# Window attention and two MoE layers on one core: whole 32-bit float scores for every unit, and a first batch that keeps its probabilities and values whole

## The chip, the cores and the metric

One NeuronCore of a Trainium2 chip runs the whole program. The metric is the device time of one execution in microseconds; lower is better. Between two kernels of this size a difference of under 0.5% (some 4.6 us) counts here as no change.

## The reference, cut to what matters

```python
batch, n_heads, seq_l, seq_g, head_dim = 4, 8, 512, 32, 64      # window = 32
k_all, v_all = concat([k_g, k_l]), concat([v_g, v_l])           # along the rows
out_g = sm(scale * q_g @ k_all.T) @ v_all                       # 32 global rows see all rows
s_ll  = where(abs(i - j) <= window, scale * q_l @ k_l.T, -1e9)
s_lg  = scale * q_l @ k_g.T
out_l = sm(concat([s_lg, s_ll])) @ v_all                        # 512 local rows: band + global
x = concat([out_g, out_l])            # 4 * 544 = 2176 tokens of 8 * 64 = 512
x = maximum(maximum(x @ w1, x @ w2), x @ w3) @ w_out            # 512 -> 768 -> 512
x = (sigmoid(x @ w_gate) * (x @ w_val)) @ w_out2                # 512 -> 1536 -> 512
```

The attention is in 32-bit floats. The MoE weights arrive as 64-bit floats (two 32-bit words each) and are turned into 32-bit floats on the chip.

## The kernel before, in words

**Units and chunks.** The attention is cut into 32 units `t`: batch `b` (4), half of the 512 local rows (2), pair of heads `hp` (4). Four units make a chunk `c` (256 rows, and in every second half the 32 global rows too: 288 columns). Chunk `c` then goes through the first MoE layer: `moe1_l1` (18 weight tiles, w1, w2 and w3 by six blocks `f`) and `moe1_l2` (w_out, six tiles). After the eighth chunk the second MoE layer runs in six chunks of 384 columns.

**A float as two.** Most matmuls take a float as a high part and a rest, and sum three products (high x high, high x rest, rest x high: `TERMS`, `mm3`). Making such a pair costs a cast on ScalarE and a subtraction on VectorE or GpSimd. Only chunk 0's first layer (`WHOLE1`, `WHOLE2`) takes 32-bit floats whole (names `xw`, `hw`, `wraw`).

**A unit's steps.** `at_prep_rows` (units 0 to 7, from row-major q and k, turned by TensorE transposes `tq`, `tk`) or `at_prep_qk` (units 8 to 31, turned on VectorE) makes the pairs `qs` and `ks`. `at_scores` runs 12 matmuls of 64 rows x 224 columns into `sp` (two heads in the two halves of the array's rows), `at_scores_g` three of 256 columns into `sg` (and three of 32 in the first half). `at_softmax` gives `sm`, splits it into `pc` in 16-bit floats (three casts on ScalarE L604, three subtractions on VectorE L607) and has a DMA transpose it into `pt` (L610). `at_prep_v` splits the values in three 16-bit parts `vb` (ScalarE L509, GpSimd L511 and L515, VectorE L513). `at_av` multiplies: 40 matmuls of 64 columns and four of 256. For each pair of head pairs `at_softmax_g` and `at_av_g` do the same for the global rows (`pcg`, `ptg`, `og`).

**Order and buffers.** Every function is a generator of small steps, and the list `ORDER` says in which order all steps of the program are emitted. Each engine and each DMA queue takes its instructions strictly in that order. All loads but chunk 0's k go through SyncE's queue (SP), and so do the DMA transposes, so that one waiting there holds up the loads behind it. The pool `slot` has `NSLOT` = 25 buffers of 4 KB per partition; it holds q, k and v rows of the first batch (`qn`, `kn`, `kx`, `vrg`), raw weights (`wraw`) and weight pairs (`w`), 24 of the latter in the end. `conv_w` loads a weight tile (L224, L227) and turns it into floats (L231 to L240). Chunk 0 uses the raw tile; the pair is made from it afterwards (L246, and a subtraction on GpSimd under L218).

## Time and profile before

| what | value |
|---|---|
| time, median of 3 runs (lowest, highest) | 913.1 us (911.05, 914.78) |
| the profiled execution: time, span of its trace | 913.18 us, 911.5 us |
| TensorE busy (matmul) | 849.0 us, 93% of the span |
| VectorE, ScalarE, GpSimd busy | 455.5, 436.6, 295.4 us |
| share of TensorE in the chain that ended last | 78% |

The span is the time from the first to the last instruction of the profiled execution. A busy share is an average over stages with different limits, and a matmul's busy time includes its latency, so back-to-back matmuls overlap in it. `L12` is line 12 of the kernel.

### The profile page before, as it was taken

The page shows a single profiled execution, that of the slowest core. Times are in us where ns is not written, and L with a number is a line of the kernel's source. Part 1 is how long each engine was busy: PE and PEld are TensorE (multiplying, and loading weights), DVE is VectorE, ACT ScalarE, POOL GpSimd, SP SyncE. Part 2 cuts the span into 40 slices and gives each one's busy share as a digit, 9 for nine tenths or more (in the row PEclk, how much of TensorE's full clock was granted, in tenths as well). Part 3 has the DMA queues.
Part 4 walks back from the last instruction along what each step waited for, and adds up shares of the span by engine and source line. Part 5 has one row for each costly group of instructions (what it writes and reads, how often), then busy time and mean ns, then how long its engine had stood idle before and what let it go on. Part 6 is the DMA issues. An engine that isn't in the chain of part 4 may idle for free.

```text
span 911.5 us, 18123 instructions
## 1 busy us (share of the span) xinstructions
PE 849.0 (93%) x7004; PEld 786.1 (86%) x7004; DVE 455.5 (50%) x1092; ACT 436.6 (48%) x1141; POOL 295.4 (32%) x284
## 2 busy tenths in 40 slices
PE   0759959999999998999999999999999999999998
PEld 0547749899999998999999999999999999999997
DVE  4797967776577776855476673121111111111211
ACT  4776658676666766664596753221211211211122
POOL 4554427644545463624265653000100100000000
PEclk9988989999999999999999999999999999999999
DMA  7687744566553646645777210000100200000000
GB/s 210 130 185 205 174 80 85 102 97 104 101 97 85 105 91 116 119 88 122 246 260 244 88 34 31 33 29 9 61 1 1 64 1 1 13 36 1 1 35 24
DMA packets 205031, 79.91 MB, mean 88 GB/s; under 512 B 171792, under 2 KB 200464, under 8 KB 204944
## 3 DMA queue, kind: packets, MB, share of 16 engines
q1 hardware_dynamic: 202288, 78.09, 36.5%
q8 instruction: 55, 0.90, 0.4%
q10 hardware_dynamic: 2656, 0.66, 0.4%
q14 instruction: 32, 0.26, 0.1%
HBM read 54.59 MB, written 8.91 MB: 70 GB/s over the span
## 4 chain that ended last, share of the span: by engine, by line
PE 78%; DVE 7%; DMA 6%; ACT 4%; SPq 2%; issue 2%; POOL 0%; DVEq 0%; POOLq 0%; ACTq 0%
PE acc L861 16%; PE ps L261 8%; PE ps L263 7%; PE ps L262 7%; PE pg L262 5%; PE pg L263 5%; PE pg L261 5%; PE pv L261 5%; PE pv L263 5%; PE pv L262 5%; DMA wraw<-in_moe_w_dram 3%; PE ot L659 2%; PE sp L538 2%; DVE pc L607 1%; DVE wraw L240 1%
## 5 line engine op out<-in xcount | busy, mean ns | idle before, releaser
L261 PE MATMUL ps<-xt,w 128*128 128x288 f32 (+1 forms) x504 | 150.1, 298 | 2.5 <-ACT h L744 1.7
L861 PE MATMUL acc<-w,gt 128*128 128x512 f32 x612 | 150.6, 396 | 0.0
L263 PE MATMUL ps<-xt,w 128*128 128x288 f32 (+1 forms) x504 | 147.2, 292 | 0.0
L262 PE MATMUL ps<-xt,w 128*128 128x288 f32 (+1 forms) x504 | 146.0, 290 | 0.1
L861 PEld LDWEIGHTS acc<-w,gt 128*128 128x128 f32 x612 | 114.1, 188 | 23.7
L846 ACT CAST gt<-sig 128x384 fp32r<-128x384 f32 (+1 forms) x72 | 35.7, 496 | 173.5 <-PE acc L861 124.2
L848 DVE TENSOR_TENSOR gt<-sig,gt 128x384 fp32r<-128x384 f32 (+1 forms) x72 | 41.7, 582 | 152.6 <-ACT gt L846 152.6
L843 DVE TENSOR_TENSOR sig<-pv,sig 128x384 f32<-128x384 f32 (+1 forms) x72 | 38.1, 534 | 155.3 <-PE pv L263 118.9
L218 POOL TENSOR_TENSOR w<-wraw,w 128x512 fp32r<-128x512 f32 x60 | 83.1, 1397 | 78.2 <-ACT w L246 74.7
L218 POOL TENSOR_TENSOR x<-x2r,x 128x384 fp32r<-128x384 f32 (+1 forms) x24 | 25.7, 1077 | 253.4 <-ACT x L824 253.4
L261 PEld LDWEIGHTS ps<-xt,w 128*128 128x128 f32 x504 | 95.4, 189 | 7.9 <-ACT h L744 2.6
L262 PEld LDWEIGHTS ps<-xt,w 128*128 128x128 f32 x504 | 95.5, 190 | 0.5 <-DVE xt L725 0.3
L263 PEld LDWEIGHTS ps<-xt,w 128*128 128x128 f32 x504 | 95.3, 189 | 0.0
L261 PE MATMUL pv<-x,w 128*128 128x384 f32 (+1 forms) x288 | 93.9, 326 | 0.4 <-DVE sig L843 0.4
L263 PE MATMUL pv<-x,w 128*128 128x384 f32 (+1 forms) x288 | 93.9, 326 | 0.0
L263 PE MATMUL pg<-x,w 128*128 128x384 f32 (+1 forms) x288 | 93.9, 326 | 0.0
L262 PE MATMUL pg<-x,w 128*128 128x384 f32 (+1 forms) x288 | 93.9, 326 | 0.0
L262 PE MATMUL pv<-x,w 128*128 128x384 f32 (+1 forms) x288 | 93.9, 326 | 0.0
L261 PE MATMUL pg<-x,w 128*128 128x384 f32 (+1 forms) x288 | 93.9, 326 | 0.0
L607 DVE TENSOR_TENSOR pc<-sm,pc 64x512 f16<-64x512 f32 (+1 forms) x96 | 69.7, 726 | 5.5 <-ACT pc L604 4.2
L841 ACT ACTIVATE sig<-pg 128x384 f32<-128x384 f32 (+1 forms) x72 | 33.8, 473 | 76.9 <-PE pg L263 42.7
L575 ACT ACTIVATE sm<-sm,st 128x224 f32<-128x224 f32 x128 | 60.7, 477 | 8.9 <-DVE st L544 8.8
(124 smaller groups left out, 1785.5 us busy)
## 6 DMA issues: line engine op xcount, KB each, us to landing
wraw<-in_moe_w_dram SPq DMA_DIRECT2D x18, 512.0 KB, 4.9
wraw<-in_moe_w_out_dram SPq DMA_DIRECT2D x18, 512.0 KB, 4.6
wraw<-in_moe_w_gate_dram SPq DMA_DIRECT2D x12, 512.0 KB, 5.8
wraw<-in_moe_w_val_dram SPq DMA_DIRECT2D x12, 512.0 KB, 8.4
vr<-in_v_l_dram SPq DMA_DIRECT2D x48, 96.0 KB, 2.5
out_dram<-o SPq DMA_DIRECT2D x17, 256.0 KB, 2.2
x2d<-x2s SPq DMA_DIRECT2D x32, 128.0 KB, 2.4
x2r<-x2d SPq DMA_DIRECT2D x20, 192.0 KB, 2.5
```

The lines of the kernel that those rows point to most:

```text
L218: nc.gpsimd.tensor_tensor(out=out, in0=a, in1=f32(b), op=ALU.subtract)
L261: nc.tensor.matmul(ps, lhsT=wh, rhs=xh, start=first, stop=False)
L262: nc.tensor.matmul(ps, lhsT=wh, rhs=xl, start=False, stop=False)
L263: nc.tensor.matmul(ps, lhsT=wl, rhs=xh, start=False, stop=last)
L538: nc.tensor.matmul(sp[hh][:, j, 0:224], lhsT=qs[r, a, qc], rhs=ks[r, k, kc], start=(i == 0), stop=(i == 2))
L575: nc.scalar.activation(sm4[:, i], sm4[:, i], AF.Exp, bias=st[:, 0, i:i + 1], scale=-1.0, accum_out=st[:, 2, i:i + 1])
L607: nc.vector.tensor_tensor(out=l_, in0=s_, in1=h_, op=ALU.subtract)
L841: nc.scalar.activation(sg[:, 0:n], pg[:, 0:n], AF.Sigmoid)
L843: nc.vector.tensor_tensor(out=sg[:, 0:n], in0=pv[:, 0:n], in1=sg[:, 0:n], op=ALU.mult)
L846: nc.scalar.copy(gt[:, 0, 0:n], sg[:, 0:n])
L848: nc.vector.tensor_tensor(out=gt[:, 1, 0:n], in0=sg[:, 0:n], in1=f32(gt[:, 0, 0:n]), op=ALU.subtract)
L861: nc.tensor.matmul(acc[ci, i], lhsT=gt[:, l, c], rhs=w[:, m], start=(f == 0 and l + m == 0), stop=(f == NF2 - 1 and l == 1))
```

## The change

It does five things.

- **Scores (all units).** `qs` and `ks` are whole 32-bit floats. Each score product is one matmul in place of three: `at_scores` has 4 in place of 12, `at_scores_g` 1 or 2 in place of 3 or 6. The pairs are not made any more: for units 0 to 7 a copy on VectorE and three on ScalarE take q and k out of PSUM, for units 8 to 31 the transposed tiles are used as they are.
- **First batch (units 0 to 7).** The probabilities stay whole floats. TensorE transposes them, eight 128 x 128 transposes a unit into two PSUM tiles `tp`; ScalarE copies one to SBUF, VectorE the other (`pw`). `at_av` is eight whole matmuls of 128 columns on the loaded values `vrg`; `at_prep_v` does nothing there. The global rows go the same way (five transposes, `at_av_gw`, 20 matmuls of 32 columns for a pair), with the values loaded once more (`at_load_vg`, `vrw`).
- **Loads.** The first batch's values are loaded in another layout, seven transfers for four heads in place of five.
- **`NSLOT`** is 26. Buffer counts of `qs`, `ks` go to 2 and 3.
- **`ORDER`** is a new list.

```diff
-    1857, 1858, 1859, 1860, 0, 1861, 1836, 1822, 1871, 1872, 1, 1823, 2, 1824, 1873, 1874, 1843, 1844, 1837, 3, 1838,
...
-    NSLOT = 4 * NF1 + 1
+    NSLOT = 4 * NF1 + 2
...
+    def at_load_vg(hp):
+        vr = at.tile([P, 5, 2, D], F32, tag="vb", name="vrw", bufs=3)
+        vl = v_l[0, 2 * hp:2 * hp + 2]
+        dma = nc.sync.dma_start
+        dma(out=vr[0:32, 0], in_=v_g[0, 2 * hp:2 * hp + 2].rearrange("h s d -> s h d"))
+        dma(out=vr[32:128, 0], in_=vl[:, 0:96, :].rearrange("h r d -> r h d"))
+        for hh in range(2):
+            dma(out=vr[:, 1:4, hh], in_=vl[hh, 96:480, :].rearrange("(k r) d -> r k d", r=P))
+        dma(out=vr[64:96, 4], in_=vl[:, 480:512, :].rearrange("h r d -> r h d"))
+        u[hp, "vrw"] = vr
...
-        qs = at.tile([P, 2, HS], F32R, tag="qs", name="qs")
-        nc.scalar.copy(qs[:, 0], tq[:, 0:HS])
-        yield
-        ks = at.tile([P, 2, 384], F32R, tag="ks", name="ks", bufs=2)
-        for o, i in parts(ks[:, 0, :]):
+        qs = at.tile([P, HS], F32, tag="qs", name="qw", bufs=2)
+        nc.vector.tensor_copy(qs, tq[:, 0:HS])
+        yield
+        ks = at.tile([P, 384], F32, tag="ks", name="kw", bufs=3)
+        for o, i in parts(ks):
             nc.scalar.copy(o, i)
-        yield
-        nc.vector.tensor_tensor(out=qs[:, 1], in0=tq[:, 0:HS], in1=f32(qs[:, 0]), op=ALU.subtract)
-        yield
-        for (o, i), (h, _) in zip(parts(ks[:, 1, :]), parts(ks[:, 0, :])):
-            nc.vector.tensor_tensor(out=o, in0=i, in1=f32(h), op=ALU.subtract)
...
-            for i, (a, k) in enumerate(TERMS):
-                for hh in range(2):
-                    r = slice(64 * hh, 64 * hh + 64)
-                    nc.tensor.matmul(sp[hh][:, j, 0:224], lhsT=qs[r, a, qc], rhs=ks[r, k, kc], start=(i == 0), stop=(i == 2))
+            for hh in range(2):
+                r = slice(64 * hh, 64 * hh + 64)
+                nc.tensor.matmul(sp[hh][:, j, 0:224], lhsT=qs[r, qc], rhs=ks[r, kc], start=True, stop=True)
...
+        if t < NGRP * NP:
+            tp = []
+            for hh in range(2):
+                tp.append(ps_o.tile([P, 2 * HS], F32, tag="ot", name="tp"))
+                for i in range(4):
+                    e = sm4[:, 2 * hh + i // 2, 96 * (i % 2):96 * (i % 2) + P]
+                    nc.tensor.matmul(tp[hh][:, P * i:P * i + P], lhsT=e, rhs=ident, start=True, stop=True, is_transpose=True)
+                yield
+            pt = u[t, "pt"] = [at.tile([P, 2 * HS], F32, tag=x, name="pw", bufs=2) for x in ("pc", "pt")]
+            nc.scalar.copy(pt[0], tp[0])
+            yield
+            nc.vector.tensor_copy(pt[1], tp[1])
+            yield
+            return
...
+        if t < NGRP * NP:
+            vr = u.pop((t, "vr"))
+            for j in range(2):
+                for i, n in ((0, 96), (1, P)):
+                    for hh in range(2):
+                        k = 2 * j + i
+                        nc.tensor.matmul(ob[64 * hh:64 * hh + 64, P * j:P * j + P], lhsT=vr[0:n, k, hh, :],
+                                         rhs=pt[hh][0:n, P * k:P * k + P], start=(k == 0), stop=(k == 3))
```

Two places show what the new order does. The first is SP's queue at the program's start. Before (`wraw` are raw weight tiles, `qn`, `kn`, `kx` q and k rows, `qgr` and `vgr` global rows, `pt` the transposed probabilities):

```order
L224 DMA wraw<-in_moe_w_dram 128x4x256 x4
L324 DMA qgr<-in_q_g_dram 32x4x32 x4
L327 DMA vgr<-in_v_g_dram 32x8x64 x3
L224 DMA wraw<-in_moe_w_dram 128x4x256 x2
L370 DMA qn<-in_q_l_dram 128x2x64 x2
...
L370 DMA qn<-in_q_l_dram 128x8x64 x2
L610 DMA_TRANSPOSE pt<-pc 128x12x128
L376 DMA kx<-in_k_l_dram 32x8x64
L377 DMA kx<-in_k_g_dram 32x8x64
L379 DMA kn<-in_k_l_dram 128x8x64 x2
L610 DMA_TRANSPOSE pt<-pc 128x12x128
L224 DMA wraw<-in_moe_w_dram 128x4x256 x3
```

The same queue after the change (`vrg` are value rows):

```order
L372 DMA qn<-in_q_l_dram 128x2x64 x2
L325 DMA qgr<-in_q_g_dram 32x4x32 x4
L372 DMA qn<-in_q_l_dram 128x6x64 x2
L225 DMA wraw<-in_moe_w_dram 128x4x256 x3
L372 DMA qn<-in_q_l_dram 128x8x64 x2
L378 DMA kx<-in_k_l_dram 32x8x64
L379 DMA kx<-in_k_g_dram 32x8x64
L381 DMA kn<-in_k_l_dram 128x8x64 x2
...
L405 DMA vrg<-in_v_g_dram 32x4x64 x2
L225 DMA wraw<-in_moe_w_dram 128x4x256 x4
```

The eighth to tenth raw weight tiles stood behind two DMA transposes and now stand behind loads alone; the first q rows, which stood behind six raw weight tiles and the global rows, are now the queue's first row.

The second place is TensorE's program around the scores of the first units. Before (`sp` local scores, `sg` global scores, `tq`, `tk` transposes of q and k):

```order
L437 MATMUL tq<-ident,qn 128x128 x2
L437 MATMUL tk<-ident,kn 128x128 x2
L437 MATMUL tk<-ident,kx 128x64
L538 MATMUL sp<-ks,qs 128x224 x12
L556 MATMUL sg<-ks,qgz_82 64x256 x3
L559 MATMUL sg<-ks,qgz_82 64x32 x3
```

After (`tp` is the transposed probabilities in PSUM, `ot` the product with the values):

```order
L467 MATMUL tq<-ident,qn 128x128 x2
L467 MATMUL tk<-ident,kn 128x128 x2
L467 MATMUL tk<-ident,kx 128x64
L611 MATMUL tp<-ident,sm 128x128 x4
L698 MATMUL ot<-pw,vrg 64x128 x8
L611 MATMUL tp<-ident,sm 128x128 x4
L554 MATMUL sp<-kw,qw 128x224 x4
L571 MATMUL sg<-kw,qgz_82 64x256
```

The twelve score matmuls of a unit are four, and between them stand the transposes `tp`, which need VectorE's `sm` before them and copies by ScalarE and VectorE behind them.

## Rows read from the trace of the kernel before

**Rows 1.** Busy time by stage: stretch, length, each engine's busy us, clock, DMA.
```profile
0.00:16.60 16.60, 0.00 (x0) 0.01 (x1) 4.49 (x9) 7.12 (x12) 9.32 (x30) 1.00 0.76 218
16.60:66.00 49.40, 28.69 (x258) 21.14 (x258) 41.46 (x115) 36.50 (x113) 23.43 (x17) 0.93 0.76 160
66.00:119.00 53.00, 46.38 (x397) 38.11 (x398) 44.56 (x102) 37.53 (x98) 23.22 (x20) 0.94 0.78 186
119.00:145.10 26.10, 17.32 (x220) 14.73 (x218) 17.98 (x51) 13.87 (x39) 10.76 (x9) 0.87 0.35 68
145.10:183.00 37.90, 35.63 (x312) 33.96 (x312) 29.98 (x84) 28.01 (x83) 25.90 (x25) 0.95 0.50 95
183.00:425.00 242.00, 238.86 (x2990) 225.43 (x2989) 171.74 (x499) 156.14 (x481) 118.16 (x117) 1.00 0.54 98
425.00:500.00 75.00, 74.71 (x615) 73.38 (x614) 43.64 (x68) 49.80 (x100) 36.14 (x30) 1.00 0.78 248
500.00:911.50 411.50, 407.40 (x2224) 379.31 (x2222) 101.71 (x171) 107.64 (x219) 48.48 (x40) 1.00 0.08 26
```

**Rows 2.** First matmuls of chunk 0's first layer and of chunk 1, by line.
```profile
L736 PE MATMUL ps<-xw,wraw x144: 379/379/792, 68.0 to 116.8; 128*128 128x256 f32 x144
...
L261 PE MATMUL ps<-xt,w x12: 296/296/382, 145.1 to 149.6; 128*128 128x288 f32 x12
```

**Rows 3.** SP queue's waits before 145.1 us: total us, times, longest.
```profile
SPq L610 <- DVE pc L607: 17.2, 4, 7.0
SPq L610 <- DVE st L544: 13.8, 2, 7.4
SPq L610 <- PE ot L664: 5.4, 1, 5.4
```

**Rows 4.** Groups by line and shape: busy us, mean ns, idle before.
```profile
L607 DVE TENSOR_TENSOR pc<-sm,pc 64x512 f16<-64x512 f32 x64 | 50.1, 783 | 4.6 <-ACT pc L604 3.8
L604 ACT CAST pc<-sm 64x512 f16<-64x512 f32 x64 | 39.5, 616 | 18.1 <-DVE sm L589 14.4 <-DMA ptg<-pcg 2.3 <-DMA pt<-pc 0.7
L607 DVE TENSOR_TENSOR pc<-sm,pc 128x256 f16<-128x256 f32 x32 | 19.6, 612 | 0.8 <-ACT pc L604 0.4
L604 ACT CAST pc<-sm 128x256 f16<-128x256 f32 x32 | 13.0, 405 | 0.4
L464 DVE TENSOR_TENSOR qs<-tq,qs 128x256 fp32r<-128x256 f32 x8 | 3.3, 418 | 0.5 <-ACT qs L458 0.4
L867 ACT COPY o<-acc 128x512 f32<-128x512 f32 x17 | 9.8, 588 | 14.0 <-PE acc L861 8.6 <-DMA out_dram<-o 5.2
```

**Rows 5.** TensorE's timeline at 84 to 88 us: start, length, line.
```profile
85.00 0.99 PE L538 MATMUL sp<-ks,qs 64*128 64x224 f32 x12
85.91 0.56 PE L556 MATMUL sg<-ks,qgz 128*64 128x256 f32 x3
86.31 1.89 PE L736 MATMUL ps<-xw,wraw 128*128 128x256 f32 x8
```

**Rows 6.** TensorE's timeline from 24 to 29 us, and around 53 us.
```profile
24.54 1.41 PE L538 MATMUL sp<-ks,qs 64*128 64x224 f32 x10 [1.30 <-DVE ks L467]
...
28.20 0.69 PE L437 MATMUL tq<-ident,qn 128*128 128x128 f32 x2
28.68 0.63 PE L437 MATMUL tk<-ident,kn 128*128 128x128 f32 x2
...
53.06 1.25 PE L659 MATMUL ot<-pt,vb 128*64 128x64 f16 x40
54.15 0.39 PE L664 MATMUL ot<-pt,vs 96*64 96x256 f16 x4
```

**Rows 7.** The wait ahead of chunk 0's second layer, TensorE's timeline.
```profile
129.72 0.79 PE L772 MATMUL ps<-hw,wraw 128*128 128x256 f32 x1 [8.72 <-DVE wraw L240]
```

**Rows 8.** The page's loads: queue, count, size, us from issue to landing.
```profile
wraw<-in_moe_w_dram SPq DMA_DIRECT2D x18, 512.0 KB, 4.9
...
vr<-in_v_l_dram SPq DMA_DIRECT2D x48, 96.0 KB, 2.5
```

More of the change, by code (lines that the diff above doesn't have):

```diff
@@ L280 @@
     sgs = [at.tile([P, 640], F32, name=f"sgs{g}") for g in range(2)]
-    qgz = [at.tile([P, NP, 2, 64], F32R, name=f"qgz{g}") for g in range(2)]
+    qgz = [at.tile([P, NP, 64], F32, name=f"qgz{g}") for g in range(2)]
     ident = at.tile([P, P], F32, name="ident")
@@ L324, in at_load_g @@
                 dma(out=qgr[p0:p0 + 32], in_=q_g[b, hh::2, :, dh * 32:dh * 32 + 32].rearrange("h s i -> s h i"))
-        vgr = at.tile([96, H, D], F32, tag="eg", name="vgr")
-        for rep in range(3):
+        whole = 2 * b < NGRP
+        if not whole:
+            vgr = at.tile([96, H, D], F32, tag="eg", name="vgr")
+        for rep in range(3) if not whole else ():
             dma(out=vgr[32 * rep:32 * rep + 32], in_=v_g[b].rearrange("h s d -> s h d"))
@@ L391, in load_v_rows @@
         r0 = 64 * (4 * half + full) - 32
-        if nh > 2:
-            for s in range(3):
-                dma(out=vr[:, :, full + s, :], in_=vl[:, r0 + 64 * s:r0 + 64 * s + P, :].rearrange("h r d -> r h d"))
-        for hh in range(nh) if nh == 2 else ():
+        for hh in range(nh):
             base = vl[hh, r0:r0 + P, :]
@@ L634, in at_softmax_g @@
         yield
+        if 2 * b < NGRP:
+            tp = [ps_o.tile([P, 2 * HS], F32, tag="ot", name="tpg") for i in range(2)]
+            for i in range(5):
+                nc.tensor.matmul(tp[i // 4][:, P * (i % 4):P * (i % 4) + P], lhsT=e[:, P * i:P * i + P], rhs=ident,
+                                 start=True, stop=True, is_transpose=True)
+            yield
+            pt = u["ptg", b, g] = at.tile([P, 640], F32, tag="pc", name="pwg", bufs=2)
+            nc.scalar.copy(pt[:, 0:512], tp[0])
+            yield
+            nc.vector.tensor_copy(pt[:, 512:640], tp[1][:, 0:P])
+            yield
+            return
         pc = at.tile([P, 2, 640], F16, tag="pc", name="pcg", bufs=2)
@@ L661, in at_av @@
                                      start=(s == 0 and i == 0), stop=False)
-        for v in range(2):
+        for v in range(2) if t >= NGRP * NP else ():
             for hh in range(2):
@@ L681, in at_av, with at_av_gw @@
         yield
+    def at_av_gw(b, g, ptg):
+        c = 2 * b + 1
+        ob = ps_o.tile([P, 2 * HS], F32, tag="ot", name="ogw")
+        for pr in range(2):
+            vr = u.pop((2 * g + pr, "vrw"))
+            for kt in range(5):
+                p0, p1 = (0, P) if kt < 4 else (64, 96)
+                for hh in range(2):
+                    r = P * kt + 32 * (2 * pr + hh)
+                    nc.tensor.matmul(ob[64 * hh:64 * hh + 64, G * pr:G * pr + G], lhsT=vr[p0:p1, kt, hh, :],
+                                     rhs=ptg[p0:p1, r:r + 32], start=(pr == 0 and kt == 0), stop=(pr == 1 and kt == 4))
+            yield
+        for pr in range(2):
+            x = xt[c, 2 * g + pr] = u.pop((c * NP + 2 * g + pr, "x"))
+            nc.scalar.mul(x[:, 0, HS:HS + G], ob[:, G * pr:G * pr + G], 1.0 / PS)
+        yield
+        for pr in range(2) if c not in WHOLE1 else ():
+            x = xt[c, 2 * g + pr]
+            nc.vector.scalar_tensor_tensor(out=x[:, 1, HS:HS + G], in0=ob[:, G * pr:G * pr + G], scalar=1.0 / PS,
+                                           in1=f32(x[:, 0, HS:HS + G]), op0=ALU.mult, op1=ALU.subtract)
+        yield
     def at_av_g(b, g):
@@ L899 @@
             once(("kg", b), t - 14, at_load_kg, b)
+        for hp in range(NP) if 2 * b < NGRP else ():
+            once(("lvg", hp), 20.0 + hp, at_load_vg, hp)
         put(("g", b), steps(t, -13.9, 3, 1, 1, 2, .1, .5, 1, .5, 1.2, .6, 1.2), at_load_g(b))
```

68 lines of the change are left out of this document (40 added, 28 removed), and 284 rows, old and new, of the table ORDER.

## The prediction

> **What bounds the kernel now.** I read the busy time by stage first, because the share of the whole (93% TensorE) hides that there are two regimes [rows 1]. From 145.1 us to the end TensorE is busy for 35.6 + 238.9 + 74.7 + 407.4 = 756.6 of 766.4 us. It idles 9.8 us there, and no other engine is above 80%. In that regime the end moves by what TensorE's own program grows or shrinks, and by nothing else. Before 145.1 us it is busy for 28.7 + 46.4 + 17.3 = 92.4 us. It does nothing for the first 16.6 us and is idle for 145.1 - 16.6 - 92.4 = 36.1 us after that. Some of the 92.4 us ran at the lower clock, 1.2 GHz: ten score matmuls take 1.41 us at 24.5 us [rows 6], twelve 0.99 us at 85.0 us [rows 5].
>
> The second view, the first matmuls by line [rows 2], gives the milestones: chunk 0's first layer runs from 68.0 to 116.8 us, and chunk 1's starts at 145.1 us. I call that moment the hand-over: from there on TensorE always has something to do. So the question splits in two: when the hand-over comes, and how much TensorE's work after it changes.
>
> The third view, the SP queue's waits [rows 3], says why the start is slow. Before 145.1 us SP stood for 17.2 + 13.8 + 5.4 = 36.4 us in seven waits in front of the DMA transposes of the probabilities (L610). All loads of weights stand behind those in the same queue. The last of these delays shows in the timeline as an 8.72 us wait for w_out's decoding (L240) ahead of chunk 0's second layer [rows 7].
>
> **The change, part by part.**
>
> *Scores after the hand-over.* TensorE's 12 matmuls of a unit are 0.91 us today (85.00 to 85.91 us, where `sg` starts), so 0.15 us for a pair of heads; the two heads run side by side, since twelve matmuls of 224 columns one behind the other would be 1.12 us at 2.4 GHz [rows 5]. A whole float costs more than one pass: chunk 0's four whole matmuls of 256 columns are eight records in 1.89 us with a latency of 0.38 us each [rows 2, 5], so (1.89 - 0.38) / 7 = 0.216 us a record, 0.43 us a matmul, which is four passes at 2.4 GHz. For 224 columns a record is then 0.19 us. The trace has no whole-float matmul on half of the array's rows, so the new cost is bounded. Lower end: four records' time with the two heads fully side by side, 0.76 us. Upper end: eight records one behind the other, 1.52 us plus 0.1 us of start. I take five records (each head's two records must follow each other, and the next head's first overlaps the last one's second), 0.95 us plus 0.1 us of start = 1.05 us, nearer to the lower end because 64-row matmuls of today do overlap. That is +0.14 us a unit, with ends -0.15 and +0.7 us. By the order of the change 21 units' scores come after the hand-over: +3 us, ends -3 and +15.
>
> The Trainium skill's page "FP8 and Floating Point Precision", section "TensorE Precision Notes", says that a true 32-bit float takes four passes through the array, against the three products that the kernel makes now; this speaks against the change. The trace agrees (four passes, 0.43 us). Scaled by passes alone, 16 in place of 12, a unit's scores would be 1.2 us, and the sum below would be 3 us longer.
>
> *Global scores.* One whole matmul of 256 columns (0.43 us) takes the place of three (0.40 us, 85.91 to 86.31 us) [rows 5]; in first halves three short ones of 32 columns become one. I count 0, ends -3 and +2 us over all units.
>
> *ScalarE, GpSimd and VectorE after the hand-over.* The casts and subtractions for `qs`, `ks` of units 8 to 31 go. None of these engines bounds that stage [rows 1], so they are worth 0 there; the cover is TensorE's own 94 to 99%.
>
> *First batch, what goes.* Per unit VectorE loses three subtractions of `pc` (2 x 0.783 + 0.612 = 2.18 us) and the one for `qs` (0.42 us); ScalarE loses the casts of `pc` (2 x 0.616 + 0.405 = 1.64 us) [rows 4], and GpSimd its passes over the values. Added are a copy of 512 columns from PSUM on ScalarE (0.59 us by the copy of `acc` [rows 4]) and one on VectorE. VectorE has no such row; between the 256 columns of L464 (0.42 us) and twice that I take 0.7 us, and 0.4 us for the copy of q. So VectorE drops by about 1.5 us net and ScalarE by 1 us a unit, over eight units 12 and 8 us. On VectorE that is about a ninth of the 108 us of work that stand before the hand-over [rows 1]. The eight DMA transposes of units and two of global rows leave SP, and with them the 36.4 us in which weights waited behind them. What comes in is 8 value loads more and 20 for `vrw`, less 3 for `vgr`; SP issues one in about 0.5 us by the queue's pace, an estimate from 96 KB loads that land in 2.5 us with several in flight [rows 8], so 12 us of issue.
>
> *First batch, what TensorE gains in work.* Two transposes of q are 0.48 us (28.20 to 28.68 us), 0.24 us each at the lower clock; at 2.4 GHz I take half of that [rows 6]. Eight for a unit: 1.9 us early, 0.96 us later; I count four units at each, 11.5 us, and 1.5 us for the global rows' ten. The products with the values are 1.48 us a unit today at the lower clock (53.06 to 54.15 + 0.39 us, 44 matmuls) [rows 6]. The new ones are 16 records of 128 columns, 0.108 us each at full speed: nine steps if the two heads overlap, 1.0 us; 16 if not, 1.7 us; against about 1.1 us now I count +0.2 us a unit, and +1.5 us for the global rows' 80 short ones. Scores of 11 units before the hand-over: +1.6 us, and by the new order one unit more of them, +1 us. Sum: 11.5 + 1.5 + 1.6 + 1.5 + 1.6 + 1 = 18.7 us, so TensorE's work before the hand-over is 92.4 + 18.7 = 111 us.
>
> *The new order at the start.* The first q rows are the head of SP's queue, no longer behind six weight tiles and the global rows, and a load of that size lands in about 2.5 us [rows 8]. TensorE's first transpose moves from 16.6 to about 6 us (ends 4 and 10).
>
> *The slot more* lets a raw weight tile be loaded while another waits to be used; it is worth something only in the w_out wait [rows 7], and is counted with the idle time below.
>
> **The sum.** Hand-over = first transpose + work + idle time = 6 + 111 + idle. Of today's 36.1 us of idle time, 8.8 us stand after 119 us (the w_out wait), 6.6 us between 66 and 119 us, and 20.7 us before 66 us [rows 1]. I let the w_out wait mostly go, because no transposes hold the queue, and halve the others, since the chain through `pc`, SP and back is replaced by one through PSUM: 14 us are left (ends 5 and 30). The hand-over then comes at 131 us (ends 120 and 147), 14 us earlier. With +3 us for scores the span is 911.5 - 14 + 3 = 900.5 us. The profiled execution took 1.7 us more than its span, and 913.18 us against a median of 913.1, so the prediction is 902 us.
>
> **The rivals.**
>
> *The two heads' whole-float matmuls don't overlap.* Then a unit's scores cost 1.6 us, 21 units 15 us in place of 3, the first batch's products with the values 5 us more, of which idle time hides some: 902 + 12 = 914 us, no change. For it: no such matmul is in the trace. Against it: the same split of the rows overlaps for the pairs of today [rows 5]. On this the Trainium skill's "TensorE: Matmul & The Clock Gate", Part 3, says that tiles in different row groups run concurrently, and doesn't tell data types apart; the trace agrees for today's operands, and no run here shows it for whole floats.
>
> *PSUM buffers take the place of SP.* The transposes need two of the three `ot` buffers for every unit, besides `sg` and `ot` itself, and each is free only when ScalarE or VectorE has copied it, behind whatever these have in their queues; VectorE is busy 84% of 16.6 to 119 us [rows 1]. TensorE runs in order, so a transpose that waits holds up the scores and chunk 0's matmuls behind it. There are 20 such tiles. At 0.7 us of wait each the early gain is gone (916 us, no change); from 0.8 us the kernel is slower by over 0.5%, and at 1.2 us, two copies' length, it is 926 us.
>
> *Loads and VectorE were the whole early limit.* VectorE's 108 us of work in 145.1 us shrink to 96 us, and the loads run without their 36.4 us of waits. Were TensorE idle for only 5 us and at full speed from about 35 us on (7 us of work less), the hand-over would be at 115 us: 16 us under the forecast, 886 us.
>
> **How the numbers follow.** I give the forecast's course 58%, serial heads 15%, PSUM 15%, the larger early gain 12%. The forecast's own range is 892 to 911: the idle time's ends and the scores' lower end, not all at once. Of it nine tenths are faster by over 0.5% (under 908.5 us). Serial heads are mostly no change, PSUM half slower. Faster: 0.52 + 0.02 + 0.02 + 0.12 = 0.68; slower: 0.03 + 0.08 = 0.11; the rest, 0.21, within. The range from 884 to 916 holds all but the upper half of PSUM's case and tails of the others, under 2 in 10.
>
> **What the changed profile would show.** Right: the first `tq` at about 6 us; no SP wait on a transpose before unit 8; chunk 1's first L261 matmul at 120 to 140 us; a unit's `sp` at 1.0 to 1.1 us in the full stage; TensorE still 97% busy after the hand-over. Wrong: `sp` at 1.5 us or more (heads in series); waits of `tp` or `sg` on ScalarE's or VectorE's copies in tens of us (PSUM); a TensorE idle again after the hand-over, because the units' supply on VectorE, now asked for earlier, comes late. That last one would give back the early gain, and the time would end near 913 us.

## The result and the profile after

The changed kernel takes 882.4 us (median of 4 runs, 881.3 to 883.4) against 913.9 us (4 runs, 911.05 to 915.8): ratio 0.966, interval 0.963 to 0.969. It is faster by 31.5 us where 11 to 12 were forecast, and ends just under the range's lower end of 884 us. The profiled execution has a span of 879.3 us.

Busy time by stage after the change. The stretches end at TensorE's first transpose, at chunk 0's first layer, at its second layer and at the hand-over; the columns are those of [rows 1].

```profile
0.00:3.54 3.54, 0.00 (x1) 0.03 (x1) 0.00 (x0) 0.00 (x0) 2.60 (x13) 1.00 0.38 81
3.54:40.30 36.76, 30.74 (x207) 21.34 (x207) 26.82 (x86) 28.53 (x94) 6.97 (x16) 1.00 1.05 262
40.30:90.10 49.80, 48.32 (x324) 39.83 (x322) 44.19 (x118) 37.56 (x104) 17.03 (x14) 1.00 0.73 187
90.10:115.60 25.50, 18.36 (x111) 14.24 (x109) 15.65 (x33) 12.62 (x39) 7.50 (x6) 0.80 0.24 53
115.60:879.30 763.70, 758.59 (x6002) 705.48 (x6000) 341.48 (x805) 322.49 (x824) 188.03 (x163) 1.00 0.30 73
```

Before the hand-over TensorE works for 30.7 + 48.3 + 18.4 = 97.4 us and idles for 6.0 + 1.5 + 7.1 = 14.6 us after its first transpose. [rows 1] had 92.4 and 36.1 us. After the hand-over it works 758.6 us and idles 5.1 us, against 756.6 and 9.8. The milestones, to compare with [rows 2]:

```profile
L810 PE MATMUL ps<-xw,wraw x144: 379/379/493, 40.3 to 87.9; 128*128 128x256 f32 x144
```
```profile
L262 PE MATMUL ps<-xt,w x504: 276/293/403, 115.6 to 437.7; 128*128 128x288 f32 x96, 128*128 128x256 f32 x72
```

Chunk 0 starts at 40.3 us in place of 68.0, and the hand-over comes at 115.6 us in place of 145.1, 29.5 us earlier. That is nearly the whole gain. TensorE's waits up to the hand-over (us, times, longest):

```profile
PE ps L846 <- DVE wraw L241: 7.1, 2, 5.9
PE tq L467 <- DMA qn<-in_q_l_dram: 3.5, 1, 3.5
PE tk L467 <- DMA kn<-in_k_l_dram: 2.2, 2, 1.3
PE sg L571 <- ACT xw L718: 1.5, 1, 1.5
PE ps L810 <- DVE wraw L241: 1.5, 1, 1.5
```

The wait for w_out's decoding [rows 7] is still there, 7.1 in place of 8.7 us, though no DMA transpose stands in SP's queue any more. The 3.5 us of `tq` lie ahead of the first transpose; all others are small. SP's two longest waits in the same stretch are a store of `x2`, the first layer's result, and a load behind the one ahead of it, no transpose:

```profile
SPq L856 <- ACT x2s L853: 13.0, 2, 12.0
SPq L225 <- DMA wraw<-in_moe_w_dram: 1.9, 2, 1.0
```

TensorE's timeline at the start, behind the wait for w_out and in the full stage:

```profile
8.49 1.87 PE L554 MATMUL sp<-kw,qw 64*128 64x224 f32 x8 [0.69 <-ACT kw L492]
...
14.35 1.86 PE L554 MATMUL sp<-kw,qw 64*128 64x224 f32 x8
...
18.86 1.03 PE L554 MATMUL sp<-kw,qw 64*128 64x224 f32 x8
19.82 0.43 PE L571 MATMUL sg<-kw,qgz 128*64 128x256 f32 x1
...
96.77 1.22 PE L846 MATMUL ps<-hw,wraw 128*128 128x256 f32 x2 [5.93 <-DVE wraw L241]
99.20 8.46 PE L846 MATMUL ps<-hw,wraw 128*128 128x256 f32 x28 [1.21 <-DVE wraw L241]
...
209.37 1.03 PE L554 MATMUL sp<-kt,qt 64*128 64x224 f32 x8
210.32 0.65 PE L571 MATMUL sg<-kt,qgz 128*64 128x256 f32 x2
```

A unit's scores hold TensorE for 0.95 us (209.37 to 210.32).

By the durations TensorE runs at 1.2 GHz until some 18 us and at 2.4 GHz from there to the wait for w_out. The clock column reads 1.00 in the first 18 us all the same: the trace has no clock record before 18.26 us, and the column counts time without one as full speed. In the old kernel the first record stands at 54.15 us. Ahead of it the matmuls take the time of the lower clock: ten scores 1.41 us at 24.5 us [rows 6] (twelve take 0.99 us at 85.0 us [rows 5]), and the three products of `sg` start 0.213 us apart, against 0.118 us at recorded full speed. So the clock of 0.93 that [rows 1] gives for 16.6 to 66 us is too high, and this stretch, for which the column reads 1.00, ran at 1.2 GHz:

```profile
16.62:54.15 37.53, 22.13 (x149) 16.54 (x151) 31.23 (x88) 27.07 (x83) 17.55 (x13) 1.00 0.77 166
```

During the wait for w_out the clock of the changed kernel falls to 1.2 GHz. 28 records behind it take 8.46 us, 0.30 us each in the mean; they start 0.427 us apart up to 103.6 us and 0.216 us apart from there on.

```profile
93.35:103.58 10.23, 5.60 (x12) 4.03 (x13) 7.15 (x14) 3.14 (x10) 1.50 (x1) 0.50 0.09 21
```

### The profile page after: what moved, and what is told of

Its sections match the earlier page's. It is cut to its first block, busy times and chain, and to the rows that moved or that the text cites. A ratio compares the mean times of both kernels' runs of the same rounds, so it can differ in the third digit from the quotient of the medians.

```text
span 879.3 us, 17150 instructions
## 1 busy us (share of the span) xinstructions
PE 856.0 (97%) x6638; PEld 780.9 (89%) x6638; DVE 428.1 (49%) x1036; ACT 401.2 (46%) x1057; POOL 222.1 (25%) x209
## 4 chain that ended last, share of the span: by engine, by line
PE 88%; DVE 4%; DMA 3%; SPq 3%; ACT 2%; issue 0%; DVEq 0%; ACTq 0%
PE acc L935 16%; PE ps L262 11%; PE ps L264 10%; PE ps L263 9%; PE pv L264 5%; PE pg L263 5%; PE pg L262 5%; PE pg L264 5%; PE pv L262 5%; PE pv L263 5%; PE sp L554 2%; PE ot L708 2%; PE ps L846 1%; PE sg L571 1%; PE ps L810 1%; DMA vrg<-in_v_l_dram 1%
## 5 line engine op out<-in xcount | busy, mean ns | idle before, releaser
L219 POOL TENSOR_TENSOR w<-wraw,w 128x512 fp32r<-128x512 f32 x60 | 87.2, 1465 | 114.7 <-ACT w L247 69.1
L920 ACT CAST gt<-sig 128x384 fp32r<-128x384 f32 (+1 forms) x72 | 35.5, 495 | 150.0 <-PE acc L935 102.7
L824 DVE TENSOR_TENSOR h<-ps,h 128x288 f32<-128x288 f32 (+1 forms) x90 | 39.1, 438 | 58.5 <-PE ps L264 48.7
```

The costliest lines, as they stand in the source:

```text
L219: nc.gpsimd.tensor_tensor(out=out, in0=a, in1=f32(b), op=ALU.subtract)
L824: nc.vector.tensor_tensor(out=a, in0=ps[:, 0:n], in1=a, op=ALU.max)
L920: nc.scalar.copy(gt[:, 0, 0:n], sg[:, 0:n])
```

## Experiments

Hand-overs below are those of the profiled execution, one for each kernel; ratios are to the kernel before, measured on the same chip. The wait of `tk` for the first k rows alone lies between 1.1 and 4.6 us in such executions of the changed kernel and its variants, so that a hand-over moved by 2 us is not clear of noise.

### What the new start is worth: the changed kernel with one delay at a time

**after_weights_first.** Seven raw weight tiles are loaded ahead of the first q rows.

```diff
 SP, first rows
+DMA wraw<-in_moe_w_dram 128x4x256 x7
 DMA qn<-in_q_l_dram 128x2x64 x2
```

> The changed kernel with its first seven weight tiles loaded ahead of q and k. Theory 'start': the first transpose moves from 3.5 us to 15 to 22 us and the hand-over (115.6 us) by at least half of that, 122 to 135 us; time 889 to 902 us. Rival 'queue' (only the waits behind DMA transposes mattered): hand-over 114 to 119 us, time 881 to 886 us.

890.7 us, ratio 0.978 (0.976 to 0.979). The first transpose came at 14.6 us, 11.1 us later, the hand-over at 125.2 us, 9.6 us later: 'start'. In the new program an early first q row counts nearly in full: of the 11.1 us 9.6 reach the hand-over.

**after_sp_waits.** A small store of the probabilities per unit stands in SP's queue, and makes it wait for VectorE as the DMA transposes did.

```diff
         if t < NGRP * NP:
+            nc.sync.dma_start(out=scr[t], in_=sm[:, 0, 0, 0:32])
             tp = []
```

> The changed kernel with one small store in the load queue for each of the first batch's eight units (128 rows of 32 floats of the probabilities, to memory that nobody reads), at the place where their transposition begins, so that the queue again waits for VectorE's result eight times. It moves hardly any bytes. Theory 'queue': the loads behind these waits come late, hand-over at 122 to 135 us instead of 115.6 us, time 889 to 902 us. Rival 'start and clock': the loads are far enough ahead, hand-over 115 to 118 us, time 882 to 885 us.

890.2 us, ratio 0.977 (0.976 to 0.979), hand-over 127.2 us: 'queue'. SP's list of waits has the stores, and the stretch from the first transpose to the hand-over shows what they cost:

```profile
SPq L607 <- DVE sm L604: 12.2, 5, 5.2
```
```profile
3.56:127.20 123.64, 101.94 (x638) 78.65 (x638) 87.62 (x232) 79.08 (x234) 31.74 (x35) 0.93 0.65 165
```

TensorE idles 21.7 us (7.1 more), and the same matmuls take 101.9 us of work (4.5 more), at a mean granted clock of 0.93. These waits are paid twice, as idle time and as slower matmuls: the trace has the clock at 1.2 GHz from 40.6 to 47.4 us, where the changed kernel's stays at 2.4.

**after_prep_late.** As in the old start, the decoding of the first five weight tiles stands ahead of the first unit's copies.

```diff
 ACT, first rows behind the loads
+ACTIVATE wraw<-wraw 128x512 x7
 COPY kw<-tk 128x64
```

> The changed kernel with the order of the old start on ScalarE and VectorE: the loads and the decoding of the first five raw weight tiles stand ahead of the first unit's copies of q and k. SP's first q rows stay first. Theory 'order' (an early first transpose counts only where the copies behind it are not behind the decoding): TensorE's first scores wait 12 to 18 us for ScalarE's or VectorE's copy, hand-over 125 to 133 us, 889 to 898 us. Rival 'slack' (other waits of the start take it up): hand-over 116 to 121 us, 882 to 886 us.

886.3 us, ratio 0.970 (0.969 to 0.972), hand-over 122.8 us, between the two theories' numbers.

```profile
PE sp L567 <- DVE qw L501: 9.5, 1, 9.5
```

The first scores wait 9.5 us for the copy of q, of which 7.2 us reach the hand-over. This wait is paid hardly more than once: TensorE idles 20.9 us after its first transpose, nearly as long as in after_sp_waits, but works for 98.6 us only, 1.2 more than in the changed kernel.

```profile
3.33:122.83 119.50, 98.60 (x639) 76.38 (x639) 87.33 (x232) 78.89 (x234) 31.54 (x36) 0.96 0.68 170
```

**after_pairs.** The casts and subtractions of the probabilities are put back, into a scratch tile that nothing reads.

```diff
                 nc.tensor.matmul(tp[hh][:, P * i:P * i + P], lhsT=e, rhs=ident, start=True, stop=True, is_transpose=True)
...
+            for d, s_ in zip(dv, sv):
+                nc.scalar.copy(d, s_)
+            for d, s_ in zip(dv, sv):
+                nc.vector.tensor_tensor(out=d, in0=s_, in1=d, op=ALU.subtract)
             yield
```

> The changed kernel with the splitting of the first batch's probabilities put back as work for nothing: per unit three casts on ScalarE (1.6 us) and three subtractions on VectorE (2.2 us) into a scratch tile that nothing reads, ahead of the copies of the transposed probabilities; over eight units 13 and 17 us before the hand-over. Theory 'chain' (that work stands in the way of the units, and what VectorE and ScalarE lost is a main part of the gain): hand-over 124 to 133 us in place of 115.6, 888 to 898 us. Rival 'slack' (as in the run with less decoding, where 16 us less for VectorE moved the hand-over by 1.2 us): hand-over 115 to 120 us, 882 to 886 us.

897.1 us, ratio 0.983 (0.982 to 0.985): 'chain'. Stages as above, from the first transpose on:

```profile
3.57:49.50 45.93, 36.61 (x207) 25.13 (x207) 35.37 (x99) 34.63 (x107) 6.37 (x16) 0.89 0.97 248
49.50:109.80 60.30, 52.88 (x324) 42.44 (x322) 53.13 (x129) 45.91 (x125) 19.17 (x15) 0.94 0.56 134
109.80:132.30 22.50, 17.64 (x112) 13.78 (x110) 13.40 (x30) 10.12 (x29) 5.50 (x5) 0.85 0.17 36
```

The hand-over comes at 132.3 us, 16.7 us later: 7.0 us of idle time and 9.7 us of work (107.1 against 97.4), though TensorE got no matmul more (207, 324 and 112 records against 207, 324 and 111). Here the clock is at 1.2 GHz from 37.6 to 47.8 us and in two more stretches. VectorE has 15.2 us more to do in these stages, ScalarE 12.0.

**after_pairs_late_sp.** The three last edits together.

```diff
 ACT
+ACTIVATE wraw<-wraw 128x512 x7
 COPY kw<-tk 128x64
...
+            nc.sync.dma_start(out=scr[t], in_=sm[:, 0, 0, 0:32])
             tp = []
...
+                nc.scalar.copy(d, s_)
...
+                nc.vector.tensor_tensor(out=d, in0=s_, in1=d, op=ALU.subtract)
```

> The changed kernel with three of the old start's delays at once: the splitting as work for nothing, the first decodings ahead of the first unit's copies (alone: hand-over 122.8 us), and the eight small stores of probabilities in SP's queue (alone: 127.2 us). Theory 'sum' (the old start is late by several such delays that add up): hand-over 135 to 148 us, close to the 145.1 of the kernel before, 898 to 912 us. Rival 'overlap' (they hide each other): hand-over 124 to 134 us, 888 to 898 us.

906.8 us, ratio 0.994 (0.992 to 0.996), hand-over 140.1 us: 'sum' by its numbers. One by one they cost 16.7, 7.2 and 11.6 us, 35.5 in all; together 24.5 us, so they overlap for 11 us. They bring back 24.5 of the 29.5 us.

### Whether the old kernel can have the early start by its order

**before_q_first.** The first q rows become the head of SP's queue, and the first k rows, which ScalarE's queue loads, go out at the start as well.

```diff
 SP, first rows
+DMA qn<-in_q_l_dram 128x2x64 x2
+DMA qn<-in_q_l_dram 128x6x64 x2
 DMA wraw<-in_moe_w_dram 128x4x256 x4
```

> The kernel before with nothing moved but the loads of the first two units' q and k to the head of the queue, ahead of the weight tiles. Theory 'start': TensorE's first transpose moves from 16.6 to 4 to 6 us, its 92 us of work before the hand-over begin 11 to 13 us earlier, and most of that reaches the hand-over (145.1 us before): 132 to 140 us, time 901 to 909 us. Rival 'queue': the hand-over is set by loads that wait behind the DMA transposes and by w_out's decoding, so the earlier start turns into idle time: hand-over 142 to 148 us, time 911 to 917 us.

916.8 us, ratio 1.005 (1.004 to 1.007), hand-over 149.5 us: theory 'start' fell, and 'queue' holds by its time, with the hand-over 1.5 us beyond its range. The first transpose comes at 3.5 us, and TensorE's timeline says where the 13 us went:

```profile
3.54 0.93 PE L450 MATMUL tq<-ident,qn 128*128 128x128 f32 x2 [3.54 <-DMA qn<-in_q_l_dram]
...
27.75 0.56 PE L551 MATMUL sp<-ks,qs 64*128 64x224 f32 x2 [18.31 <-ACT ks L475]
```

ScalarE's copy of k stands behind the decoding of weight tiles in ScalarE's own program, and these tiles are loaded later now.

**before_q_first_w_scalar.** With q first, the 24 weight tiles are loaded through ScalarE's queue.

```diff
-            nc.sync.dma_start(out=raw.rearrange("p (k f) t -> p k (f t)", k=KD),
+            wdma(out=raw.rearrange("p (k f) t -> p k (f t)", k=KD),
```

> The kernel before with the first units' q and k rows at the head of SP's queue, as in the run with q first (hand-over 149.5 us, 916.8 us), and with the loads of the first layer's 24 weight tiles on ScalarE's DMA queue, so that none stands behind a transpose of the probabilities. Theory 'queue' (weights behind SP's waits are what makes the old start slow, and with them gone the earlier start counts): TensorE's idle time after its start falls from 51 to 20 to 35 us, hand-over 120 to 134 us, 888 to 902 us. Rival 'chain' (the way through the casts, VectorE's subtractions and the transposes of the probabilities is slow by itself): hand-over 140 to 150 us, 907 to 918 us. A rival on the other side, 'ScalarE' (a load that waits there holds ScalarE's work): over 918 us.

937.7 us, ratio 1.028 (1.026 to 1.030): the rival on the other side. The first scores wait 26.9 us for ScalarE; the edit disturbs more than it frees, and says nothing on the queue.

**before_loads_first.** With q first, twelve loads are moved in front of the DMA transposes.

```diff
 SP
+DMA wraw<-in_moe_w_dram 128x4x256 x4
+DMA kx<-in_k_l_dram 32x8x64
...
 DMA_TRANSPOSE pt<-pc 128x12x128
```

> The kernel before with only its order changed: the first units' q and k rows at the head of SP's queue (as in the run with q first: hand-over 149.5 us, 916.8 us), and twelve loads (nine raw weight tiles, the second half's k rows and two groups of value rows) moved in front of the DMA transposes of the probabilities that they stood behind. The transposes themselves stay. Theory 'queue' (loads behind SP's waits make the old start slow, and with them gone the earlier start counts): TensorE's idle time after its start falls from 51 to 20 to 35 us, hand-over 118 to 134 us, 886 to 902 us. Rival 'chain' (the way of the probabilities through casts, VectorE's subtractions and the DMA transpose is slow by itself, whoever waits behind it): hand-over 140 to 150 us, 907 to 918 us.

924.1 us, ratio 1.012 (1.009 to 1.015), hand-over 154.6 us. The wait for `ks` stays (18.1 us). 'Queue' fell as the one cause; the result lies beyond the rival's range too. The hand-over is 5 us later than with q first alone: the waits for ScalarE's `ks` are 29.0 us in all in place of 25.6, and a wait of 3.7 us for VectorE's `h` is new.

**before_start_first** and **before_start_loads_first.** The first two units' copies, scores and first softmax steps are written ahead of the decoding, with q first, without and with the loads moved.

```diff
 ACT, first rows behind the loads
+CAST qs<-tq 128x256
+CAST ks<-tk 128x64
...
 ACTIVATE wraw<-wraw 128x512
```

> The kernel before with only its order changed: the first units' q and k rows at the head of SP's queue (as in the run with q first: hand-over 149.5 us, 916.8 us), and the copies, pairs, scores and first softmax steps of the first two units written ahead of the first weight tiles' decoding on ScalarE and VectorE. In the run with q first TensorE's first scores waited 18.3 us for ScalarE's copy of k, which stood behind that decoding. Theory 'order' (the old programs of ScalarE and VectorE, not SP's queue alone, keep an earlier start from counting): the 18.3 us wait goes, TensorE's idle time after its start falls from 51 to 30 to 40 us, hand-over 128 to 140 us, 895 to 907 us. Rival 'later wait' (the gain is taken back by the loads and decodings that now come later): idle 45 to 52 us, hand-over 143 to 150 us, 910 to 918 us.

919.0 us, ratio 1.008 (1.005 to 1.010), hand-over 146.6 us: 'later wait', by its hand-over (the time is 1 us over that range). TensorE's longest waits:

```profile
PE sp L551 <- ACT ks L475: 16.4, 5, 8.5
PE ps L785 <- DVE wraw L253: 8.7, 1, 8.7
PE tk L450 <- DMA kn<-in_k_l_dram: 7.7, 4, 3.4
PE sg L569 <- ACT qgz L348: 6.1, 1, 6.1
```

The 18 us wait is gone from the first unit and stands, in two or three parts, at the next ones.

> Both order edits of the kernel before together: the first two units' steps ahead of the decoding, and the twelve loads moved in front of the DMA transposes (alone: hand-over 154.6 us, 924.1 us). Theory 'both' (an old start without the ScalarE wait needs its weights sooner, so that now the loads in front of the transposes count): hand-over 120 to 132 us, 887 to 899 us. Rival 'chain' (the way of the probabilities through casts, subtractions and DMA transposes is what is left): hand-over 135 to 148 us, 902 to 916 us.

924.8 us, ratio 1.012 (1.011 to 1.014), hand-over 157.4 us, later than both theories had it. No order of the old code that was tried brought its hand-over under 146 us with an early first q row.

### Other terms

**before_whole_scores.** The kernel before with the whole-float scores alone.

```diff
-            for i, (a, k) in enumerate(TERMS):
-                for hh in range(2):
-                    r = slice(64 * hh, 64 * hh + 64)
-                    nc.tensor.matmul(sp[hh][:, j, 0:224], lhsT=qs[r, a, qc], rhs=ks[r, k, kc], start=(i == 0), stop=(i == 2))
+            for hh in range(2):
+                r = slice(64 * hh, 64 * hh + 64)
+                nc.tensor.matmul(sp[hh][:, j, 0:224], lhsT=qs[r, qc], rhs=ks[r, kc], start=True, stop=True)
```

> The kernel before with the scores part alone: whole 32-bit floats for q and k in all units, everything else and the order as before. Theory 'TensorE's cost': a unit's local scores take 0.96 us in place of 0.86 us, its global scores 0.11 to 0.17 us more, over 22 units after the hand-over 5 us; the waits of the first units' scores on ScalarE's and VectorE's pairs (12 us) fall by some us before it: time 911 to 918 us. Rival 'relief': the casts and subtractions that go free ScalarE, VectorE and GpSimd early, and the hand-over comes 6 us or more earlier: 902 to 910 us.

911.0 us, ratio 0.999 (0.997 to 1.001), no change. Its stage after the hand-over:

```profile
142.80:911.40 768.60, 761.88 (x6015) 708.31 (x6012) 341.46 (x818) 326.88 (x839) 184.80 (x162) 1.00 0.30 74
```

TensorE's work there grows by 5.3 us (756.6 before), its idle time falls from 9.8 to 6.7 us, and the hand-over comes 2.3 us earlier. The 5 us of 'TensorE's cost' came; 'relief' did not.

**before_less_decode** and **after_less_decode.** VectorE's sign step of the first layer's 24 tiles is left out; the weights lose their signs.

```diff
-        nc.vector.scalar_tensor_tensor(out=lo, in0=hi, scalar=-2147483648, in1=lo,
-                                       op0=ALU.bitwise_and, op1=ALU.bitwise_or)
+        if whole is None:
+            nc.vector.scalar_tensor_tensor(out=lo, in0=hi, scalar=-2147483648, in1=lo,
+                                           op0=ALU.bitwise_and, op1=ALU.bitwise_or)
```

> The kernel before without VectorE's step that puts the sign into the low word of the first layer's 24 raw weight tiles (L237, 17.2 us before the hand-over; the weights lose their signs). Theory 'VectorE' (it bounds the old start, as its 108 us of 145 say): hand-over 128 to 138 us in place of 145, 896 to 907 us. Rival 'queue' (VectorE has idle time there that takes up whatever it saves): hand-over 141 to 146 us, 908 to 914 us.

910.2 us, ratio 0.997 (0.996 to 0.999), hand-over 142.8 us.

> The changed kernel without VectorE's step that puts the sign into the low word of the first layer's 24 raw weight tiles (L238, 17.5 us before the hand-over; the weights lose their signs). Theory 'VectorE' (the changed kernel's hand-over is now set by VectorE, 24.7 of 25 us busy from 75 to 100 us): the 7.1 us of waits ahead of the second layer's matmuls go, these run at full speed, hand-over 103 to 110 us in place of 115.6, 870 to 877 us. Rival 'TensorE' (97 us of work from 3.5 us on, with 15 us of idle time spread over the whole start): hand-over 112 to 116 us, 879 to 883 us.

880.3 us, ratio 0.964 (0.962 to 0.966), hand-over 114.4 us. Some 17 us less for VectorE are worth 2.3 and 1.2 us, as the rivals had it: its amount of work bounds neither start. In the second the order still puts w_out's last decoding step late:

```profile
PE ps L847 <- DVE wraw L242: 5.2, 2, 4.6
```

**after_decode_act.** Six low words are decoded on ScalarE in place of VectorE.

```diff
-    LOW_ACT_A = set(range(0, 4 * NF1, 2))
+    LOW_ACT_A = set(range(0, 4 * NF1, 2)) | set(range(13, 4 * NF1, 2))
```

> The changed kernel with the low part of six raw weight tiles (each odd one from the 13th on, three of them of w_out) decoded on ScalarE in place of VectorE. Theory 'VectorE sets the end of the start' (24.7 of 25 us busy from 75 to 100 us, ScalarE 13 to 17): six times 0.64 us leave VectorE before the hand-over, which comes 2 to 4 us earlier, 878.5 to 880.5 us. Rival 'TensorE' (its work and the order bound the hand-over): 882 to 884 us. Rival 'ScalarE' (the low part waits there behind softmax work): hand-over later, 884 to 888 us.

886.4 us, ratio 0.972 (0.970 to 0.974), hand-over 121.4 us: the rival 'ScalarE' by its numbers. That the low part's wait is the cause is not shown: the waits that grew are one of 2.2 us for ScalarE's `h` (L818) and the one for the first k rows, 4.1 in place of 2.2 us, and the clock falls once more, from 61.5 to 65.0 us.

**after_warm.** Eleven dummy products around the first unit's transposes.

```diff
+        warm(4)
         tq = ps_mm.tile([P, CH], F32, tag="mm", name="tq")
```

> The changed kernel with eleven dummy whole-float products of the identity on TensorE around the first unit's transposes, so that TensorE is busier before its full clock comes (at about 18 us in the changed kernel; a unit's scores 1.87 us before, 1.03 us after). Their results are not used. Theory 'clock' (TensorE's work before the hand-over shrinks when the full clock comes earlier): the dummies end before 10 us, the scores at 8 and 14 us take about 1.0 in place of 1.87 us, work other than the dummies falls by 3 to 5 us, the hand-over comes 2 to 5 us earlier, 877 to 880.5 us. Rival 'supply' (what TensorE gains at the start becomes idle time behind VectorE and the loads, as in the kernel before with q first): idle time rises by as much, hand-over at 115 to 117 us, 881.5 to 884 us.

884.3 us, ratio 0.970 (0.967 to 0.972), hand-over 117.8 us.

```profile
9.86 1.87 PE L565 MATMUL sp<-kw,qw 64*128 64x224 f32 x8
16.03 1.84 PE L565 MATMUL sp<-kw,qw 64*128 64x224 f32 x8
19.62 1.03 PE L565 MATMUL sp<-kw,qw 64*128 64x224 f32 x8
```

The dummies brought the full pace only half a microsecond sooner (the first clock record stands at 17.73 us), and the clock fell again from 24.6 to 28.0 us, so neither theory was put to the test. They delayed the first scores by 1.4 us.

**after_fill** and **after_fill_first.** Dummy products meant for the wait for w_out's decoding. The first run has them in block 0 of the second layer, but block 3 is written first; the second run has them behind the first product of block 3, and the diff is its own.

```diff
+            if c == 0 and m == 3 and f == 1:
+                for _ in range(10):
+                    nc.tensor.matmul(wm[:, 0:n], lhsT=ident, rhs=hold["h", 0][:, 0, 0:n], start=True, stop=True)
             if c in WHOLE2:
```

> The changed kernel with twelve dummy whole-float products of 256 columns on TensorE in the 5.9 us in which it waits for w_out's decoding (L241) at 90.8 us; their results are not used. The records of chunk 0's second layer behind that wait take 0.30 us each in place of 0.22 us (28 in 8.46 us). Theory 'clock' (the wait lowers the clock, and that costs behind it): those records fall to 0.22 to 0.25 us, the hand-over comes 1.5 to 2.5 us earlier, 879.5 to 881 us. Rival 'decoding' (the second layer goes at the pace of w_out's decoding): the records wait instead, no change, 882 to 884 us.

891.2 us, ratio 0.977 (0.975 to 0.979), hand-over 122.6 us. The dummies stood behind the wait and added 5.8 us to the path, so neither theory was put to the test.

> The changed kernel with ten dummy whole-float products of 256 columns (4.3 us at full speed) on TensorE right behind the first product of chunk 0's second layer, so inside its 5.9 us wait for w_out's decoding; their results are not used. In the run with twelve of them they stood behind the wait and took 5.8 us of the path; the records behind them took 0.22 us, those ahead of them 0.47 us. Theory 'clock' (the wait lowers the clock, and that costs behind it): the records after the wait take 0.22 to 0.25 us in place of 0.30 in the mean, hand-over 1.5 to 3 us earlier, 878.5 to 881 us. Rival 'decoding' (the second layer goes at the pace of w_out's decoding whatever the clock): no change, 881.5 to 884 us. Rival on the other side (the dummies outlast the wait or run at half speed): over 885 us.

883.1 us, ratio 0.967 (0.965 to 0.969), no change: 'decoding'.

```profile
91.91 4.48 PE L849 MATMUL wm<-hw,ident 128*128 128x256 f32 x20
98.01 0.71 PE L851 MATMUL ps<-hw,wraw 128*128 128x256 f32 x2 [1.63 <-DVE wraw L241]
100.44 8.03 PE L851 MATMUL ps<-hw,wraw 128*128 128x256 f32 x28 [1.72 <-DVE wraw L241]
```

With TensorE kept busy, the product behind the wait takes 0.71 us in place of 1.22, and then waits for the next tile. The 28 records are hardly faster (8.03 against 8.46 us), as the clock still falls, for 3.4 in place of 10.2 us.

## Why the prediction was off

**What was right.** The split at the hand-over held. The first transpose came at 3.5 us, just under its ends of 4 to 10, and SP no longer stands at a DMA transpose. The scores are 0.95 us a unit against 1.05 forecast. Two of the rivals did not come: whole-float heads run side by side, and no `tp` or `sg` waits long for a copy.

**What was right by luck.** The idle time is 14.6 us where 14 were forecast, but the forecast let the w_out wait mostly go and halved the other 27 us. The w_out wait kept 7.1 of its 8.7 us, so it does not need the transposes in the queue, and the others fell to 7.5. TensorE's work after the hand-over grew by 2.0 us where 3 were forecast for the local scores alone. With one unit fewer there, the local scores cost 0.8 us more, the global scores, counted as 0, 2.5 us more, and the rest 1.4 us less.

**The step that failed** is the sum "so TensorE's work before the hand-over is 92.4 + 18.7 = 111 us". It measured 97.4 us, 5.0 more than before. Every matmul is counted here from the end of the one before it, in both traces' records; the last column counts work at 1.2 GHz half:

| work before the hand-over, us | before | after | forecast of the difference | measured | at full pace |
|---|---|---|---|---|---|
| transposes of probabilities (`tp`, `tpg`) | 0 | 9.8 | +13.0 | +9.8 | +9.4 |
| products with the values (`ot`, `og`) | 11.9 | 10.9 | +3.1 | -1.0 | +0.6 |
| scores (`sp`, `sg`) | 22.2 | 21.0 | +2.6 | -1.2 | +3.9 |
| chunk 0's layers, `tq`, `tk` | 58.4 | 55.9 | 0 | -2.5 | +0.7 |

The added work was about right in all, though not part by part: some 14.7 us at full pace, against 18.7 with half of the transposes priced at 1.2 GHz (3.8 us of the 18.7). What was wrong is that the 92.4 us were carried over as they stood. The first paragraph of the prediction had named the lower clock in them, but took nothing out. By the traces' clock records, and by the durations ahead of the first of them, 36.8 of the 92.4 us ran at 1.2 GHz, and 17.4 us after the change:

| kernel | idle time after the first transpose, us | TensorE's work | of it at 1.2 GHz | work, that part counted half |
|---|---|---|---|---|
| before | 36.1 | 92.4 | 36.8 | 74.0 |
| the changed kernel | 14.6 | 97.4 | 17.4 | 88.7 |
| after_weights_first | 13.4 | 97.3 | 17.0 | 88.8 |
| after_prep_late | 20.9 | 98.6 | 19.8 | 88.7 |
| after_sp_waits | 21.7 | 101.9 | 25.4 | 89.2 |
| after_pairs | 21.6 | 107.1 | 33.4 | 90.4 |
| after_pairs_late_sp | 31.7 | 104.8 | 27.1 | 91.3 |

So the lower clock cost half of 36.8 us, 18.4, before and 8.7 after. These 9.7 us and the 3.8 us of the transposes are the 13.6 us by which the sum was too long, but for 0.1 us. The last column also shows that most of what the delays add to the same matmuls is the clock; what it leaves is at most 2.6 us. But the work does not simply grow with the idle time: three kernels idle for 21 to 22 us and work for 98.6, 101.9 and 107.1 us. The 9.5 us wait of after_prep_late stands ahead of its first full speed (29.4 us) and hardly changes the work; in after_sp_waits and after_pairs most of the added idle time stands behind it (23.5 and 20.5 us), and the clock falls again.

**The second step** is the relief of VectorE and ScalarE. Before the hand-over VectorE fell by 22 us where 12 were forecast (108.5 to 86.7), ScalarE by 16 where 8 were (95.0 to 78.7). The prediction left out VectorE's subtractions for `ks` (6.7 us) and the values' casts on VectorE and ScalarE (3.3 and 4.9 us). And the relief was only let into the sum as "halve the others". Put back, the probabilities' splitting alone cost 16.7 us, more than waits in SP's queue (11.6), on which the prediction had put the slow start, or the late copies (7.2), which it did not name. It isn't VectorE's total that counts: 17 us of decoding less are worth 1 to 2 us, while 15 us of splitting more cost 16.7. The splitting stands between a unit's softmax and its product. That this place makes the difference, and not also that one run takes away and the other adds to a nearly full engine, is argued, not shown.

**A reading that was too low.** SP's waits at L610 before the hand-over are 40.8 us in ten, not 36.4 in seven; three short ones for ScalarE are not in [rows 3].

**The balance.** First transpose -2.5 us, work -13.6, idle +0.6: the hand-over 15.4 us under the forecast's 131. After the hand-over 763.7 in place of 769.4 us, 5.7 less, of which 4.7 are idle time (9.8 to 5.1 us). The prediction had counted the relief of ScalarE, VectorE and GpSimd there as 0; with the scores alone 3.1 us of it come.

**The rival of the larger early gain** (hand-over 115 us, 886 us) had the right place, and the wrong mix: 5 us of idle time and 104 us of work where 14.6 and 97.4 were measured. Its idea of full speed earlier was right. Of its two causes VectorE's amount bounds neither start, and the waits in SP's queue are worth 11.6 us in the changed kernel.

**The rule on four passes** (the Trainium skill, "FP8 and Floating Point Precision", section "TensorE Precision Notes") would have made a unit's scores 1.2 us by passes alone; the trace has 0.95 us. On the row groups, the Trainium skill's "TensorE: Matmul & The Clock Gate", Part 3, is now borne out for whole floats: the eight records start in pairs 0.007 us apart and the last three pairs 0.19 us apart, so the two heads overlap.

**What stays open.** The three delays bring back 24.5 of the 29.5 us. What the other 5 us are (the pairs of q and k, the values' splitting, the rest of the new order) was not separated. Nor is it shown what makes the clock rise at one time or another: no run changes the clock and nothing else, and the mean granted clock of the old kernel's executions lies between 0.968 and 0.992, so its course is not the same each time. The 26th slot alone, the new code in the old order and the old code in the new order were not tried.

## What to carry to other kernels

Before old work is carried into a sum, ask at what clock it ran, by the durations of a known shape: here 18 of the 92 us of the old start were the price of the lower clock, and half of that went with the change. Price added matmuls at the pace that they will have after the change. Where several engines run written-out programs in order, a transfer that is moved forward can be worth nothing until the copies behind it are moved as well, and here even that was not enough; look for the first wait that takes its place. To learn what a removed step was worth, put it back into the new kernel as work for nothing: it told more here than all edits of the old one.

## What the runs showed of the hardware

- The granted-clock column reads 1.00 where a trace has no clock record, which is before 18.3 us in the changed kernel and before 54.2 us in the old one. The durations are those of 1.2 GHz there: eight score records take 1.87 us ahead of 18.3 us and 1.03 us from 18.9 us on, and transposes of the probabilities start 0.213 us apart ahead of it and 0.109 us behind.
- In all eight traces of the old code 32 to 46 us of TensorE's work up to the hand-over run at 1.2 GHz, in the eleven of the new code 14 to 33 us.
- TensorE being busy for 7.3 of the first 10 us in place of 3.5 (after_warm) moved the first record of full speed by half a microsecond, from 18.3 to 17.7 us.
- Two heads' whole-float matmuls of 64 rows overlap: eight records of 224 columns hold TensorE for 0.95 us.
